# Spectral mixing and a SiLU block on one core: loads moved behind the first batch's third stage, and its stand-in products made narrow

## The chip, the cores and the metric

The kernel runs on 1 core of one Trainium2 chip. The metric is the device time of one execution in microseconds (us); lower is better. The core has a matrix engine (TensorE, PE in the profile, with its weight loads listed as PEld), VectorE (DVE), ScalarE (ACT), GpSimd (POOL) and SyncE (SP), which only issues transfers. Transfers are issued by SP, ACT or POOL and carried out by 16 DMA engines.

## The reference

Two blocks follow each other. The first mixes each channel along the sequence with a filter in the frequency domain; the second is a two-layer block with a SiLU.

```python
# x: (8, 3008, 256); filt_r, filt_i: (1505, 256)
X = np.fft.rfft(x, axis=1)
Y = X * (filt_r + 1j * filt_i)[None]
y = np.fft.irfft(Y, n=3008, axis=1).astype(np.float32)
# x: (24064, 256); w_in: (256, 2048); w_out: (2048, 256)
h = y.reshape(24064, 256) @ w_in
out = ((h / (1 + np.exp(-h))) @ w_out).astype(np.float32)
```

## The kernel before, in words

**The Fourier part** is done by small matrix products, batch by batch (B = 8), with the sequence length split as 47 x 64. Stage one (products `pa`, tiles `t1`) transforms over 94 rows, stage two (`pb`, a multiplication by the filter, `pc`) over the rest and back, stage three (`pd`) back over the rows into the tile `y` that the second block reads. Between stages the data change their layout by a trip through DRAM (`d1`, `d2`).

**The second block** runs in steps. There are 8 batches x 2 halves x 3 groups of tokens, and 8 steps (`jp`) to each group, 384 steps. `hidden(step)` makes seven products with the first weights (`px`, `pyz`, L977), the sums on VectorE and the SiLUs on ScalarE; `project(step)` makes seven products with the second weights (`acc`, L1044) one step later. Both use a scheme with seven products in place of eight, for which combinations of the weights are formed on the chip (`combine_weights`). All products are in float32; each appears in the trace as two multiplies and two weight loads.

**The weights** come as 64-bit numbers and are turned into float32 on the chip, one tile j of 16 at a time: `weights(j)` loads, `bits` takes exponent and mantissa apart (VectorE), `converted` shifts the exponent (ScalarE), `added`/`signed` (together `rounded`) and `placed` put the number together (VectorE). Step jp needs tiles 2 jp and 2 jp + 1, so that tiles 0 to 7 are prepared before the first step and 9 to 15 during the steps 0 to 6.

**The order** is written out by hand (a manual schedule): each engine carries out its instructions in the order in which the program issues them. Ahead of the steps stands a start of some 70 us, in which batch 0 goes through its stages one to three alone. `forward(0, fill=4)` puts four stand-in products in front of its own, whose result is overwritten; `idle(n)` and `idle_wide(n)` issue n stand-ins into a bank of their own, 128 or 256 columns wide. At its end the program stands like this (L1341 on): load of weight tile 9; stage-one products of batch 1 for u = 0 and 1 (`second["stage1"]`, of eight u); loads of x for u = 2 and 3 and of the weight tiles 10, 11, 12; the rest of the weight tiles 4 to 7; a copy on POOL into `gate` which holds POOL until tile 7 is placed, and behind it `store_rows`, eight transfers of t1 to d1; fifteen wide stand-ins; `stage3(g)` for g = 0 to 3, 32 products each, with their copies into y; two wide stand-ins; the load of a table `wi_t` which stage three has read until then.

From there on, work beside the steps is placed by `put(step, round, piece)`, with eight rounds to a step: the pieces are issued between the products of that step. The other `stage1(u)`, u = 2 to 7, of batch 1 stand in round 3 of the steps 0 to 5. Each issues two products (512 columns, L416), the load of x for u + 2 on SP, two copies on ScalarE (L421) into one of two `t1` buffers, and the four transfers of `store_rows` on POOL. Of d1, batch 1's stage two reads from step 10 on.

Of the kernel before, what the change touches and what calls it, by code (L numbers as in the profile page):

```python
# [263 lines left out]
def kernel(  # L264
# [9 lines left out]
    nc = tc.nc  # L274
# [65 lines left out]
    y = {}  # L340
# [18 lines left out]
    def spectral(b):  # L359
# [155 lines left out]
        def forward(g, home=(None, None), fill=0):  # L515
            t2 = None if b == 0 else t2s.pop(g)
            ps = [bank(b, f"pb_{b}_{g}_{k}", home[k]) for k in range(2)]
            for _ in range(fill):
                nc.tensor.matmul(out=ps[0][:, 0], lhsT=wx_t, rhs=wide_rows, start=True, stop=True)
            for ri in range(2):  # L520
                for j in range(4):
                    for k in range(2):
                        par, at = slot_source(k, j)
                        rows = slice(64 * par, 64 * par + 64)
                        rhs = us["t2"][rows, 2 * g + at // 2, :, at % 2] if b == 0 else t2[rows, at, :]
                        nc.tensor.matmul(out=ps[k][32 * j:32 * j + 32, ri, :],  # L526
                                         lhsT=d_t[rows, 4 * g + at, ri, :], rhs=rhs,
                                         start=True, stop=True)
            if b > 0 and g + 2 < NG:
                load_t2(g + 2)  # L530
            banks[g] = ps
            prods[g] = []
# [263 lines left out]
    def put(step, rnd, piece, *args):  # L796

        pending.append((step + rnd / ROUNDS, len(pending), lambda: piece(*args)))
# [3 lines left out]
    def plan(b, part):  # L802

        at = STEPS * b

        if b == 1:
            for u in range(2, 8):
                put(at + u - 50, 3, part["stage1"], u)
        else:
            put(at - {2: 80, 3: 120}.get(b, 128), 0, part["reverse_x"])  # L810
            early_fold = (-73, ((-68, 3), (-68, 5), (-67, 5), (-66, 5))), (-89, ((-82, 5), (-81, 3), (-81, 5), (-75, 5)))
            for f, step, load, places, ends in (
                    (0, -64, *early_fold[b > 2], ((1, 0), (1, 3))),
                    (1, -56, -63, ((-61, 5), (-60, 3), (-60, 5), (-59, 3)), ((1, 3), (2, 3))),
                    (2, -48, -55, ((-52, 3), (-52, 5), (-51, 5), (-50, 5)), ((1, 3), (2, 3)))):
                put(at + load, 4 if load == -89 else 0, part["load_fold"], f)
                for k, (fold_step, rnd) in enumerate(places):
                    put(at + fold_step, rnd, part["fold"], f, k)
                put(at + step, 7, part["stage1_fold"], f)
                put(at + step, 7, part["evict_fold"], f)  # L820
                for q, (after, rnd) in enumerate(ends):
                    put(at + step + after, rnd, part["pairs_fold"], f, q)
                joined.add(at + step)
                opened.add(at + step + 1)
            put(at - 47, 0, part["load_fold"], 3)
            for k, (step, rnd) in enumerate(((-45, 3), (-45, 5), (-44, 3), (-44, 5))):
                put(at + step, rnd, part["fold"], 3, k)
            early_out.add(at - 43)
            open_step(at - 43, (part["stage1_fold"], 3), (part["evict_fold"], 3))
            put(at - 43, 3, part["pairs_fold"], 3, 0)  # L830
            put(at - 43, 5, part["pairs_fold"], 3, 1)
            return plan_two(b, part)
        put(at - 38, 0, part["load_t2"], 0)
        put(at - 38, 0, part["load_t2"], 1)
        for g, places in enumerate((
# [6 lines left out]
            pieces = (("forward", g), ("multiply", g, 0), ("multiply", g, 1), ("add", g, 0), ("add", g, 1))  # L842
            for (step, rnd), (piece, *args) in zip(places, pieces):
                if piece != "forward" or g in (1, 3, 5):
                    put(at + step, rnd, part[piece], *args)
        open_step(at - 36, *last_part[0](5), (part["forward"], 0))
        for g, step in ((0, -32), (2, -24), (4, -16)):
            put(at + step, 7, part["inverse"], g, 2)
            if g < 4:
                pending.append((at + step + 7 / ROUNDS, 10 ** 6 + 9, lambda g=g: part["forward"](g + 2, ACCS)))  # L850
                joined.add(at + step)
            put(at + step, 7, part["even"], g, 0, 2)
            put(at + step, 7, part["even"], g, 1, 2)
            put(at + step + 1, 5, part["rows"], g, 0, 2)
            put(at + step + 2, 3, part["rows"], g, 1, 2)
        plan_rest(b, part)
# [325 lines left out]
    def add_weights(*js):  # L1182

        for j in js:
            lo, m, mo = raws[j][0], raws[j][3], raws[j][5]
            v.scalar_tensor_tensor(out=mo, in0=lo, scalar=2.0 ** -32, in1=m, op0=ALU.mult, op1=ALU.add)

    def round_weights(*js):
        for j in js:
            hi, e, eo = raws[j][1], raws[j][2], raws[j][7]  # L1190
            v.scalar_tensor_tensor(out=eo, in0=hi, scalar=0x80000000, in1=e,
                                   op0=ALU.bitwise_and, op1=ALU.bitwise_or)
# [24 lines left out]
    def weights(*js, queue=None):  # L1217
        for j in js:
            if wide:
                load_weights(j, queue)  # L1220
# [9 lines left out]
    def split(*js):  # L1230
        bits(*js)
        converted(*js)

    def rounded(*js):
        if wide:
            add_weights(*js)
            round_weights(*js)
# [25 lines left out]
    def idle_wide(n, ps=None, rhs=None):  # L1263

        ps = ps or bank(0, "idle")
        for _ in range(n):
            nc.tensor.matmul(out=ps[:, 0], lhsT=wx_t, rhs=wide_rows if rhs is None else rhs,
                             start=True, stop=True)
# [28 lines left out]
        part["stage1_first"](j)  # L1297
    second["load_two"]()
    weights(8)
    part["forward"](0, fill=4)  # L1300
    placed(0, 1)
    for g in range(1, 4):
        part["forward"](g)
# [37 lines left out]
    weights(9)  # L1341
    for u in range(2):
        second["stage1"](u, False)
    second["load_x"](2)
    weights(10)
    second["load_x"](3)
    weights(11, 12)
    converted(6, 7)
    converted(8)
    rounded(4, 5)  # L1350
    placed(4, 5)
    rounded(6, 7)
    placed(6, 7)
    gp.tensor_copy(out=gate, in_=w_t[:, 3, S3, 0, 0:1])
    for u in range(2):
        second["store_rows"](u)
    idle_wide(15)
    for g in range(4):
        part["stage3"](g)
    idle_wide(2)  # L1360
    nc.sync.dma_start(out=wi_t, in_=wi_dram.ap())
    early[0] = None
    plan_rest(0, part)
    for g in (4, 5):
# [3 lines left out]
        put(step, 0, lambda t=t, dram=dram: nc.sync.dma_start(out=t, in_=dram.ap()))  # L1368
    for b in range(1, B):
        plan(b, second if b == 1 else spectral(b))  # L1370
    def added(*js):
        if wide:
            add_weights(*js)

    def signed(*js):
        if wide:
            round_weights(*js)

    for step, rnd, *todo in (
            (0, 1, (combine_weights, 1)), (0, 5, (bits, 9), (added, 9)),  # L1380
            (1, 0, (converted, 9)), (1, 1, (added, 8), (signed, 8), (placed, 8), (signed, 9), (bits, 10)),
            (1, 2, (weights, 13)), (1, 5, (combine_weights, 2), (converted, 10)),
            (2, 1, (placed, 9), (added, 10), (signed, 10), (placed, 10), (bits, 11)),
            (2, 2, (weights, 14, 15)), (2, 5, (combine_weights, 3), (converted, 11)),
            (3, 1, (combine_weights, 4), (added, 11), (signed, 11), (bits, 12)),
            (3, 5, (placed, 11), (converted, 12)),
            (4, 1, (combine_weights, 5), (added, 12), (signed, 12), (placed, 12)),
            (4, 5, (bits, 13), (added, 13)), (5, 0, (converted, 13)),
            (5, 1, (bits, 14), (added, 14), (signed, 13), (placed, 13)),
            (5, 5, (combine_weights, 6), (converted, 14)), (5, 7, (bits, 15)), (6, 0, (converted, 15)),  # L1390
            (6, 1, (signed, 14), (placed, 14), (added, 15), (signed, 15), (placed, 15)),
            (6, 5, (combine_weights, 7))):
        for piece, *args in todo:
            put(step, rnd, piece, *args)
# [79 lines left out]
```

## Time and profile before

| | us |
|---|---|
| median of 3 runs | 2510.78 |
| lowest and highest run | 2509.8, 2512.3 |
| the profiled execution, its time | 2512.45 |
| the profiled execution, its span | 2510.7 |
| PE busy | 2488.4 (99%) |
| DVE busy | 1756.2 (70%) |
| ACT busy | 1095.5 (44%) |

The span is the time from the first to the last instruction of the core in the one execution that the profiler recorded; that execution's own time is 1.75 us longer. All times inside the execution are counted from the start of the span. A row of the timeline gives start, length, engine, line, operation, what is written and read, shapes, the number of instructions merged into the row and, in brackets, how long the engine had been idle before and what ended that. "issue" stands where the profile shows nothing that the engine waited for.

### The profile page before, as it was taken

To read this page: it belongs to the slowest core of one execution; us is meant where nothing else is said; L and a number is where in the kernel's file an instruction comes from. 1 tells how busy PE (TensorE), PEld (TensorE's weight loads), DVE (VectorE), ACT (ScalarE), POOL (GpSimd) and SP (SyncE) were. 2 spreads that over 40 slices of the span, in tenths; PEclk is the share of its full clock that TensorE was granted. 3 is DMA by queue.
4 is the path that set the end of the run, shared out by engine and by line. 5 is a ranking of instruction groups with operands and counts; after the bars stand their busy time and mean duration, and the time that the engine had idled before them with its cause. 6 is when DMAs were issued, how large, how long until landed. Compare 5 with 4: busy or idle time off the path is not lost.

```text
span 2510.7 us, 42210 instructions
## 1 busy us (share of the span) xinstructions
PE 2488.4 (99%) x16206; PEld 2133.9 (85%) x16206; DVE 1756.2 (70%) x3603; ACT 1095.5 (44%) x3006; POOL 431.0 (17%) x673
## 2 busy tenths in 40 slices
PE   8999999999999999999999999999999999999999
PEld 5688888888888888888888888888888888888988
DVE  7766777777777777777777767777677766655544
ACT  3544444444444444444444444444444444444443
POOL 3102212022121121211222112211121111101100
PEclk9999999999999999999999999999999999999999
DMA  9413232312332032420324203321042211200000
GB/s 324 147 50 95 69 92 59 81 51 73 67 86 78 27 81 59 104 70 16 93 61 109 59 25 80 86 70 43 26 109 59 55 43 34 63 21 9 17 9 17
DMA packets 139801, 170.67 MB, mean 68 GB/s; under 512 B 20860, under 2 KB 113372, under 8 KB 138716
## 3 DMA queue, kind: packets, MB, share of 16 engines
q1 hardware_dynamic: 115536, 120.77, 18.3%
q0 software_dynamic: 22080, 44.10, 6.8%
q8 instruction: 127, 2.08, 0.3%
q10 hardware_dynamic: 1984, 3.11, 0.3%
q14 instruction: 74, 0.61, 0.1%
HBM read 96.06 MB, written 81.26 MB: 71 GB/s over the span
## 4 chain that ended last, share of the span: by engine, by line
PE 97%; DVE 1%; DMA 1%; issue 0%; ACT 0%; SPq 0%; POOL 0%; DVEq 0%; ACTq 0%
PE acc L1044 45%; PE px L977 26%; PE pyz L977 19%; PE pd L754 1%; PE pf L486 1%; PE pc L582 1%; PE pb L544 1%; PE pa L392 0%; PE pa L416 0%; DMA w_t<-in_x_first_dram 0%; PE pd L718 0%; DMA w_t<-d 0%; DVE g L948 0%; PE pb L526 0%; PE pc L640 0%
## 5 line engine op out<-in xcount | busy, mean ns | idle before, releaser
L1044 PE MATMUL acc<-g,w_t 128*128 128x256 f32 (+1 forms) x5376 | 1508.2, 376 | 3.0 <-ACT o L767 2.5
L1044 PEld LDWEIGHTS acc<-g,w_t 128*128 128x128 f32 x5376 | 1017.5, 190 | 152.6 <-ACT o L767 15.3
L948 DVE TENSOR_TENSOR g<-pyz,abc 128x256 f32<-128x256 f32 (+1 forms) x1152 | 479.3, 416 | 483.3 <-ACT abc L998 241.2
L948 DVE TENSOR_TENSOR g<-g 128x256 f32<-128x256 f32 (+3 forms) x1152 | 589.7, 512 | 196.6 <-ACT g L981 183.5
L977 PE MATMUL px<-ty,w_t 128*128 128x256 f32 (+1 forms) x2304 | 676.7, 375 | 0.5 <-ACT abc L998 0.5
L981 ACT ACTIVATE g<-g 128x256 f32<-128x256 f32 (+1 forms) x1152 | 472.9, 411 | 236.9 <-DVE g L948 236.9
L948 POOL TENSOR_TENSOR s<-s 128x256 f32<-128x256 f32 (+1 forms) x329 | 252.1, 784 | 1427.5 <-DVE s L1062 1094.1
L977 PEld LDWEIGHTS px<-ty,w_t 128*128 128x128 f32 x2304 | 434.8, 190 | 56.9 <-issue 3.7
L977 PE MATMUL pyz<-y,w_t 128*128 128x256 f32 (+1 forms) x1536 | 452.1, 376 | 2.3 <-DVE g L948 2.2
L977 PEld LDWEIGHTS pyz<-y,w_t 128*128 128x128 f32 x1536 | 283.7, 189 | 46.0 <-DVE g L948 6.5
L992 ACT COPY abc<-px 128x256 f32<-128x256 f32 (+1 forms) x384 | 141.3, 368 | 373.4 <-PE px L977 373.4
L981 ACT ACTIVATE g<-px 128x256 f32<-128x256 f32 (+1 forms) x384 | 145.8, 380 | 299.7 <-PE px L977 299.7
L998 ACT COPY abc<-px 128x256 f32<-128x256 f32 (+1 forms) x384 | 141.5, 368 | 308.6 <-PE px L977 308.5
L977 PE MATMUL px<-y,w_t 128*128 128x256 f32 (+1 forms) x768 | 228.0, 379 | 0.0
L977 PE MATMUL pyz<-ty,w_t 128*128 128x256 f32 (+1 forms) x768 | 226.4, 377 | 0.2
L977 PEld LDWEIGHTS px<-y,w_t 128*128 128x128 f32 x768 | 143.8, 190 | 23.3 <-ACT g L981 2.5
L977 PEld LDWEIGHTS pyz<-ty,w_t 128*128 128x128 f32 x768 | 142.3, 190 | 21.8 <-DVE g L948 1.8
L985 ACT COPY abc<-px 128x256 f32<-128x256 f32 (+1 forms) x384 | 135.1, 352 | 36.1 <-PE px L977 36.1
L506 POOL DMA_DIRECT2D d<-tf x96 | 48.6, 506 | 216.3 <-DVE tf L436 210.8
L1062 ACT COPY s<-acc 128x512 f32<-128x512 f32 (+1 forms) x94 | 54.2, 577 | 47.6 <-issue 29.1
L603 POOL DMA_DIRECT2D d<-low x36 | 22.3, 618 | 286.3 <-DVE low L599 286.2
L476 DVE TENSOR_TENSOR uf<-x_all 120x512 f32<-120x512 f32 (+1 forms) x72 | 60.2, 864 | 0.3 <-issue 0.3
(132 smaller groups left out, 1356.5 us busy)
## 6 DMA issues: line engine op xcount, KB each, us to landing
t<-d SPq DMA_DIRECT2D x84, 256.0 KB
t<-d SPq DMA_DIRECT2D x224, 96.0 KB
out_dram<-s SPq DMA_DIRECT2D x64, 256.0 KB
d<-q POOLq DMA_DIRECT2D x48, 256.0 KB, 5.2
x_all<-in_x_dram SPq DMA_DIRECT2D x96, 96.0 KB
x_all<-xr SPq DMA_DIRECT2D x96, 96.0 KB
d<-tf POOLq DMA_DIRECT2D x96, 96.0 KB, 2.7
d<-tq POOLq DMA_DIRECT2D x96, 96.0 KB, 2.9
```

The costliest lines, as they stand in the source:

```text
L476: nc.vector.tensor_tensor(out=out, in0=in0, in1=in1, op=op)
L486: nc.tensor.matmul(out=ps[q][32 * k:32 * k + 32], lhsT=wq_t[rows, k], rhs=rhs[k][rows], start=True, stop=True)
L506: nc.gpsimd.dma_start(out=d1[par, :, grp, at:at + 4], in_=part[rows].rearrange("p q n c -> p (q n) c"))
L544: nc.tensor.matmul(out=ps[k, ri][32 * j:32 * j + 32, a, :], lhsT=dn_t[rows, 4 * (g + a) + at, :], rhs=t2s[g + a][rows, at, :], start=True, ...
L948: eng.tensor_tensor(out=out, in0=in0, in1=in1, op=op)
L977: nc.tensor.matmul(out=out, lhsT=w_t[:, jp, c, 0], rhs=rhs, start=start, stop=True, skip_group_check=True)
L981: nc.scalar.activation(out=g[:, k, 0:n], in_=g[:, k, 0:n] if src is None else src, func=AFT.Silu)
L985: nc.scalar.copy(out=sums[:, 0, 0:n], in_=xo)
L992: nc.scalar.copy(out=sums[:, 1, 0:n], in_=xo)
L998: nc.scalar.copy(out=sums[:, 2, 0:n], in_=xo)
L1044: nc.tensor.matmul(out=acc[pair][i][:, h, 0:n], lhsT=w_t[:, jp, OUT_PLACE.get(c, c), 1], rhs=g[:, k, 0:n], start=(jp == 0 and h == 0), sto ...
L1062: copy(out=s[:, 2 * i:2 * i + 2, 0:n], in_=acc[pair][i][:, :, 0:n])
```

## The change

- The loads of x for u = 2 and 3 and of the weight tiles 10, 11, 12 are issued behind stage three of batch 0, after the load of `wi_t`, in the order x(2), weights 10, 11, 12, x(3).
- Weight tile 8's `added` and `signed` are issued ahead of stage three (on VectorE in front of the copies into y); before, they stood in step 1.
- Thirty narrow stand-ins stand in front of stage three in place of fifteen wide ones; one wide one behind it in place of two; eight narrow fillers in front of `forward(0)` in place of four wide ones.
- The copy into `gate` reads a column of y that stage three's last copy writes, and stands, with the eight transfers of `store_rows` behind it, after stage three.
- `stage1(u)` of batch 1 for u = 2 to 7 stands in the steps 1 to 6 in place of 0 to 5.

```diff
@@ forward
             for _ in range(fill):
-                nc.tensor.matmul(out=ps[0][:, 0], lhsT=wx_t, rhs=wide_rows, start=True, stop=True)
+                nc.tensor.matmul(out=ps[0][:, 0, 0:128], lhsT=wx_t, rhs=wide_rows[:, 0:128], start=True, stop=True)
@@ plan
             for u in range(2, 8):
-                put(at + u - 50, 3, part["stage1"], u)
+                put(at + u - 49, 3, part["stage1"], u)
@@ the start
-    part["forward"](0, fill=4)
+    part["forward"](0, fill=8)
...
     weights(9)
     for u in range(2):
         second["stage1"](u, False)
-    second["load_x"](2)
-    weights(10)
-    second["load_x"](3)
-    weights(11, 12)
     converted(6, 7)
     converted(8)
     rounded(4, 5)
     placed(4, 5)
     rounded(6, 7)
     placed(6, 7)
-    gp.tensor_copy(out=gate, in_=w_t[:, 3, S3, 0, 0:1])
+    added(8)
+    signed(8)
+    idle(30)
+    for g in range(4):
+        part["stage3"](g)
+    gp.tensor_copy(out=gate, in_=y[0, 0][:, 0, 28:29])
     for u in range(2):
         second["store_rows"](u)
-    idle_wide(15)
-    for g in range(4):
-        part["stage3"](g)
-    idle_wide(2)
+    idle_wide(1)
     nc.sync.dma_start(out=wi_t, in_=wi_dram.ap())
+    second["load_x"](2)
+    weights(10, 11, 12)
+    second["load_x"](3)
     early[0] = None
...
-            (1, 0, (converted, 9)), (1, 1, (added, 8), (signed, 8), (placed, 8), (signed, 9), (bits, 10)),
+            (1, 0, (converted, 9)), (1, 1, (placed, 8), (signed, 9), (bits, 10)),
```

More of the change, by code (lines that the diff above doesn't have):

```diff
@@ L1232, in split, with added, signed @@
         converted(*js)
+    def added(*js):
+        if wide:
+            add_weights(*js)
+    def signed(*js):
+        if wide:
+            round_weights(*js)
     def rounded(*js):
@@ L1370 @@
         plan(b, second if b == 1 else spectral(b))
[L1371 to L1377, printed above, removed]
     for step, rnd, *todo in (
             (0, 1, (combine_weights, 1)), (0, 5, (bits, 9), (added, 9)),
-            (1, 0, (converted, 9)), (1, 1, (added, 8), (signed, 8), (placed, 8), (signed, 9), (bits, 10)),
+            (1, 0, (converted, 9)), (1, 1, (placed, 8), (signed, 9), (bits, 10)),
             (1, 2, (weights, 13)), (1, 5, (combine_weights, 2), (converted, 10)),
```

## The prediction

> **What bounds the kernel now.** I read the page first, then PE's waits over the whole span, then the chain of waits around the longest of them.
>
> ```profile
> PE 2488.4 (99%) x16206; PEld 2133.9 (85%) x16206; DVE 1756.2 (70%) x3603; ACT 1095.5 (44%) x3006; POOL 431.0 (17%) x673
> PE pd L718 <- issue: 5.5, 1, 5.5
> PE idle L1261 <- DMA wx_t<-wx_tbl: 4.8, 1, 4.8
> PE acc L1044 <- ACT o L767: 2.5, 3, 0.8
> PE pyz L977 <- DVE g L948: 2.2, 4, 0.9
> ```
>
> PE is busy 99% of the span, and apart from the start there is one wait above 0.9 us: 5.5 us in front of a stage-three product (pd, L718), put down to "issue", that is to nothing the profile shows. What is saved before the steps begin is therefore kept, because PE runs without a gap worth naming from then on. The chain of waits there (start, length, what):
>
> ```profile
> 52.76 3.84 DMA w_t<-d
> 56.74 2.63 PE pd L718 x161
> 59.36 5.48 issue
> 64.85 2.81 PE pd L718 x92
> 73.17 1.88 PE pa L416 x4
> ```
>
> Stage three of batch 0 waits for its rows (w_t<-d), runs 161 products, stops 5.48 us, and runs the last 92 at nearly double the cost of one. The windows (PE busy, PEld, DVE, ACT, POOL, granted clock, DMA share, GB/s) and the DMA view say why:
>
> ```profile
> 56.70:59.40 2.70, 2.63 (x161) 2.53 (x161) 1.77 (x3) 1.66 (x5) 0.81 (x2) 1.00 0.97 269
> 59.40:64.80 5.40, 0.00 (x0) 0.00 (x0) 0.00 (x0) 0.34 (x1) 3.60 (x8) 0.84 1.03 274
> 64.80:67.60 2.80, 2.75 (x94) 2.66 (x94) 0.55 (x1) 0.47 (x1) 0.00 (x0) 0.50 0.92 357
> 69.40:77.10 7.70, 7.18 (x19) 4.07 (x17) 3.51 (x11) 2.88 (x8) 1.16 (x2) 0.74 0.13 36
> q8 instruction: 127, 2.08, 0.3%
> q8 instruction: 1, 0.02, 16.8%
> q8 instruction: 1, 0.02, 12.1%
> ```
>
> In the hole no compute engine but POOL works, the DMA engines are full (1.03), and the clock falls to 0.50 and stays low into step 0 (0.74). Queue q8 moved 127 packets of 2.08 MB: 16.4 KB each. Each product is two weight loads and two multiplies; counting those and one instruction per extra wait, PE's stream is 32,620 instructions, so a packet is a block of 256. The second and third q8 rows are the windows 61.5 to 62.0 and 66.0 to 66.5: one block arrives inside the hole, the next right behind it. By that count stage three begins at 1,148 and the hole lies at 1,480. The block before that edge begins at 1,224: 76 instructions, or 36 multiplies, into the stage, which is near 57.1. So I read it as a late block: asked for at 57.1, begun at 61.75, usable at 64.85, 7.75 us in all, behind the loads of x and weights and POOL's stores.
>
> [...]
>
> **The change, part by part.** The sum is made on the profiled execution, 2512.45 us (span 2510.7); the median of the three runs is 2510.78, and the difference is taken off that.
>
> *Stand-ins.* Fifteen wide ones go, thirty narrow ones come:
>
> ```profile
> 49.18 6.64 PE L1267 MATMUL idle<-d_t,wx_t 96*128 96x256 f32 x30
> 4.78 7.66 PE L1261 MATMUL idle<-wx_t 96*128 96x128 f32 x36 [4.78 <-DMA wx_t<-wx_tbl]
> 11.95 0.30 PEld L1261 LDWEIGHTS idle<-wx_t 96*128 96x128 f32 x2
> 12.06 0.19 PEld L1261 LDWEIGHTS idle<-wx_t 96*128 96x128 f32 x1
> 12.17 0.28 PE L1261 MATMUL idle<-wx_t 96*128 96x128 f32 x1
> ```
>
> A wide half takes 6.64/30 = 0.22 us. Narrow ones at the start take 7.66/36 = 0.213, but their last loads, 0.19 long, start 0.11 apart (11.95, 12.06) and the multiplies follow at 12.06 and 12.17: that is the warm pace. Sixty halves at 0.108 are 6.5 us, so PE is free near 55.7, as before, with 60 instructions more. The eight narrow fillers in front of forward(0) likewise last as long as four wide ones and add 16. Together 76: stage three now begins at 1,148 + 76 = 1,224, on a block's edge, and its 516 instructions are two blocks and 4 instructions. Cost 0; if the warm pace were false, see the first rival.
>
> *Loads behind stage three.* SP now issues, after the weights of tile 9, the table wi_t, which waits for stage three's last product, and behind it x(2), weights 10, 11, 12, x(3). So these 2.3 MB (five transfers by the rows below) no longer compete with the last w_t<-d rows or with the instruction blocks; POOL's eight stores, gated on the last y copy, also move behind. Terms:
>
> The rows landed at 56.60; between the cover's end at 55.7 and 56.7 I take a start at 56.3: −0.4 (0 to −1.1). The hole goes: −5.48. The 92 products at 2.81 (30.5 ns) run as the first 161 (2.63, 16.3 ns): −1.3. New waits for blocks: one edge lies at the start of stage three, asked for some 0.9 us earlier while stand-ins run; the next is passed 256 instructions on, about 2.1 us later, and its successor is needed after another 2.1. When the hole ended at 64.85 the next packet began at 66.0, 1.15 later; the packet itself is 0.121 × 16 × 0.5 = 1.0 us; so a block takes at least 2.2 us, and by the 3.1 from packet to use in the hole at most 4.2. Against 2.1 to 3.0 available I take +0.9 in all (0 to 2.1).
>
> *pa products one step later.* Step 0 had pa and its two evictions in it:
>
> ```profile
> 71.47 0.42 DVE L948 TENSOR_TENSOR g<-pyz,abc 128x256 f32<-128x256 f32 x1 [1.48 <-PE pyz L977]
> 75.96 0.43 DVE L948 TENSOR_TENSOR g<-pyz,abc 128x256 f32<-128x256 f32 x1 [2.61 <-ACT abc L998]
> 77.70 0.42 DVE L948 TENSOR_TENSOR g<-pyz,abc 128x256 f32<-128x256 f32 x1
> 99.09 1.02 PE L1044 MATMUL acc<-g,w_t 128*128 128x256 f32 x4
> 107.13 1.02 PE L1044 MATMUL acc<-g,w_t 128*128 128x256 f32 x4
> 114.89 1.02 PE L1044 MATMUL acc<-g,w_t 128*128 128x256 f32 x4
> 121.64 1.03 PE L1044 MATMUL acc<-g,w_t 128*128 128x256 f32 x4
> 124.39 0.70 PE L977 MATMUL pyz<-y,w_t 128*128 128x256 f32 x2 [0.86 <-DVE g L948]
> ```
>
> Step 0 hangs on DVE, whose third sum at 77.70 lets step 1 go on. DVE waited 1.48 for a product at half clock and 2.61 for the copy at L998 that stood behind pa's evictions. With a warm clock and no pa, both products are there before DVE, which still has the token sums and a weight combination in hand: −4.09 at most, I take −3.8 (−2.6 if the clock stays low). In return step 6 gets the seventh pa. Steps, from one group of four to the next: 8.04 with pa, 7.76 with pa (step 5), 6.75 without (step 6). So +1.3; PE time alone is 1.88, and step 7 waits 0.86 for DVE, which would shrink: 0.2 to 1.9.
>
> *Weight tile 8* is finished earlier: two DVE operations, 1.3 us, ahead of the y copies. They go into DVE's long idle before these copies (7.55 us in front of the first one): 0; if DVE ran late, at most 1.3.
>
> *Cover of the moved transfers.*
>
> ```profile
> raw<-in_moe_w_dram SPq DMA_DIRECT2D x2, 512.0 KB
> x_all<-in_x_dram SPq DMA_DIRECT2D x1, 384.0 KB
> 66.02 0.55 DVE L732 COPY y<-pd 128x376 f32<-128x376 f32 x1 [7.55 <-PE pd L718]
> 82.86 0.42 DVE L1170 TENSOR_SCALAR e<-raw 128x512 uint32<-128x512 uint32 x1
> 81.93 0.59 ACT L421 COPY t<-pa 128x512 f32<-128x512 f32 x1 [1.15 <-PE pa L416]
> 58.53 0.19 POOL L1354 COPY gate<-w_t 128x1 f32<-128x1 f32 x1 [16.12 <-DVE w_t L1198]
> 58.77 4.23 POOL L429 DMA_DIRECT2D d<-t  x8
> d<-t POOLq DMA_DIRECT2D x8, 96.0 KB, 7.6
> ```
>
> Stage three should end near 61.3. Weights 10 are then issued near 62.2 with 0.9 MB up to their end, 3.4 us at 269 GB/s, so there near 66; step 1 reads them (82.86 before, some 10 earlier now, less two operations) near 71.6. Spare: 5 us. The eviction of pa(2) in step 1 (81.93 before for step 1, near 72 now) writes the tile of t1(0), whose four stores leave POOL by 64.3 and, at the 7.6 us of loaded stores, land at 71.9. That cover is all but used: 0 expected, up to 1 us if they run longer; ACT's copies would stand behind it, and PE behind them. SP's later issues (x(4) and on, each behind a pa) shift with their steps; the rows of d1 are read from step 10 on, over two steps behind the last store.
>
> Sum: −0.4 − 5.48 − 1.3 + 0.9 − 3.8 + 1.3 = −8.8: 2503.7 on the profiled execution, **2502.0** on the median. The bounds give −11.7 to −5.4, 2499.1 to 2505.4.
>
> **Rivals.** A difference of 0.2%, 5 us, is about what a measurement of this kernel can tell from none.
>
> 1. *Narrow stand-ins cost double.* If load and multiply followed each other at the 0.213 us of the first row above, sixty halves end at 62.0, 5.7 late, and the fillers add about 1.0: −8.8 + 6.7 = −2.1, 2508.7. For it: the mean of the 36. Against: the last starts, 0.11 apart. [...] 6%.
>
> 2. *Two late blocks in place of one: slower.* If a block takes long whatever the loads do, both edges of stage three now cost a wait. At F per block the stage ends at 54.8 + 2F; at the 7.75 seen that is 70.3 against 67.66, +2.6, with a cold clock again (DVE's 2.61 saved, not the 1.48) and +1.3 for pa: about +1.3, 2512.1. It decides from F = 7.1; over 0.2% slower needs 9.6. For it: the only hole sits on an edge. Against: the packet after the hole began in 1.15 us, not 4.65, and the dense stretch below, 322 instructions in 4.0 us and so over at least one edge, has no hole. 7%, of which 2% beyond 0.2%.
>
> ```profile
> 190.71:194.75 4.04, 4.04 (x161) 2.89 (x161) 1.65 (x4) 1.95 (x4) 3.81 (x6) 1.00 0.15 61
> ```
>
> 3. *The hole is no block at all* and stays: −8.8 + 5.5 + 1.3 − 0.9 = −2.9, 2507.9. [...] The packet in the hole and the count speak against. 3%.
>
> 4. *Transfers late.* Loads and stores together starve step 1, as above; to end over 0.2% slower it must cost 14 us, against a spare of 5 and 0. 4%.
>
> **How the numbers follow.** Forecast 80%: faster by more than 0.2%, since even its upper bound is 5.4 us below. Within 0.2%: rival 1 with 6%, rival 2 with 5%, rival 3 with 3%, together 14%. Slower: 2% of rival 2 and the 4% of rival 4. Range: the forecast's bounds, cut to 2499.3 below, where every term would have to be at its end, and stretched to 2507.0 above for blocks late by more than I allow and stores late by a few us.
>
> **What would show it.** Right: pd's 256 products in one run from about 56 to 61 with pieces of at most 2 us, clock 1.00 through step 0, no 2.61 in front of DVE's sum, sixty narrow halves in 6.5 us, step 6 near 8. Wrong: stand-ins ending near 62, an "issue" wait above 3 us in pd, clock 0.50 in step 0, or ACT waiting in step 1 on the stores' queue.

## The result, and the profile after

| | before | after |
|---|---|---|
| median, us | 2512.06 (2509.8 to 2512.5, 7 runs) | 2503.14 (2502.64 to 2504.73, 7 runs) |
| the profiled execution, its time | 2512.45 | 2503.14 |
| its span | 2510.7 | 2501.4 |

The changed kernel is faster: the ratio is 0.9967, with a 95% interval of 0.9956 to 0.9979. The forecast was 2502.0 within 2499.3 to 2507.0, and 8.8 us off the profiled execution; the profiled executions differ by 9.31 and the medians by 8.92. That 2503.14 lies 1.1 above the forecast comes of the base: the median before is 2512.06 over seven runs, and the forecast started from 2510.78 over three.

First, of the changed kernel's page, the busy time of the engines:

```profile
PE 2483.7 (99%) x16242; PEld 2129.1 (85%) x16242; DVE 1756.4 (70%) x3603; ACT 1095.6 (44%) x3006; POOL 430.9 (17%) x673
```

PE's busy time fell by 4.7 us although the page lists 36 instructions more; the rest of the 9.3 is idle time that went. PE's waits (total us, times, longest):

```profile
PE pyz L977 <- DVE g L948: 1.1, 2, 0.6
PE pd L718 <- DMA w_t<-d: 1.0, 1, 1.0
PE pd L718 <- issue: 0.8, 1, 0.8
```

The wait of 5.5 in front of a pd product is now one of 0.8. Of the waits of pyz for DVE's g two are left of four, and the longest, 0.9 before, is 0.6. The chain of waits around it (start, length, what):

```profile
51.91 5.15 DMA w_t<-d
57.20 4.01 PE pd L718 x251
61.20 0.80 issue
62.00 0.33 PE pd L718 x3
...
63.01 0.70 DVE ty L948
```

251 recorded products (each one multiply, of the two that a float32 product takes) follow each other in 4.01 us, 16.0 ns each. The one wait left stands in front of the last three. By the prediction's count stage three lies on three blocks of instructions, with four instructions in the third; three multiplies and three weight loads are left, so to within two instructions this is that block's edge. The windows of the same places (PE busy, PEld, DVE, ACT, POOL, granted clock, DMA share, GB/s):

```profile
57.17:61.20 4.03, 4.00 (x251) 3.91 (x251) 2.93 (x5) 2.17 (x5) 0.00 (x0) 1.00 0.04 12
61.20:62.00 0.80, 0.00 (x1) 0.00 (x0) 0.00 (x0) 0.00 (x0) 0.00 (x0) 1.00 0.00 0
63.00:67.80 4.80, 4.08 (x15) 2.19 (x15) 4.49 (x12) 1.89 (x6) 4.39 (x9) 1.00 0.86 264
```

The DMA engines are empty during stage three (share 0.04, then 0.00) and busy in step 0 (0.86): the transfers have moved there. The clock is 1.00 throughout. The timeline of stand-ins, of DVE and ACT in the steps 0 and 1, and of the groups of four products that end the steps 5, 6 and 7:

```profile
49.06 6.86 PE L1269 MATMUL idle<-wx_t 96*128 96x128 f32 x60
66.59 0.42 DVE L948 TENSOR_TENSOR g<-pyz,abc 128x256 f32<-128x256 f32 x1 [0.16 <-ACT abc L998]
68.34 0.42 DVE L948 TENSOR_TENSOR g<-pyz,abc 128x256 f32<-128x256 f32 x1
72.86 1.15 ACT L421 COPY t<-pa 128x512 f32<-128x512 f32 x2 [1.45 <-DMA d<-t]
74.32 0.42 DVE L948 TENSOR_TENSOR g<-pyz,abc 128x256 f32<-128x256 f32 x1 [1.39 <-ACT abc L998]
105.52 1.02 PE L1044 MATMUL acc<-g,w_t 128*128 128x256 f32 x4
113.76 1.02 PE L1044 MATMUL acc<-g,w_t 128*128 128x256 f32 x4
119.95 1.03 PE L1044 MATMUL acc<-g,w_t 128*128 128x256 f32 x4
```

DVE's wait of 2.61 in front of the second sum of step 0 is 0.16. Its third sum, on which step 1 hangs, starts at 68.34 in place of 77.70: 9.36 earlier. ACT waits 1.45 in step 1 for the stores of t1, which is one of the signs that the prediction listed under "wrong"; DVE's 1.39 behind it is no longer than where ACT waited for pa itself (1.38 with ACT's wait on pa of 1.15, in the kernel with weight tile 9 behind, below), and PE shows no wait there.

### The profile page after: what moved, and what is told of

Same layout as the page of the kernel before. It is cut to its first block, busy times and chain, and to the rows that moved or that the text cites. A ratio compares the mean times of both kernels' runs of the same rounds, so it can differ in the third digit from the quotient of the medians.

```text
span 2501.4 us, 42281 instructions
## 1 busy us (share of the span) xinstructions
PE 2483.7 (99%) x16242; PEld 2129.1 (85%) x16242; DVE 1756.4 (70%) x3603; ACT 1095.6 (44%) x3006; POOL 430.9 (17%) x673
## 4 chain that ended last, share of the span: by engine, by line
PE 97%; DMA 1%; DVE 1%; ACT 0%; issue 0%; SPq 0%; POOL 0%; DVEq 0%; ACTq 0%
PE acc L1044 46%; PE px L977 26%; PE pyz L977 20%; PE pd L754 1%; PE pf L486 1%; PE pc L582 1%; PE pb L544 1%; PE pa L392 0%; PE pa L416 0%; DMA w_t<-in_x_first_dram 0%; DMA w_t<-d 0%; DMA d<-q 0%; PE pd L718 0%; PE pb L526 0%; PE pc L640 0%; DVE g L948 0%
## 5 line engine op out<-in xcount | busy, mean ns | idle before, releaser
L998 ACT COPY abc<-px 128x256 f32<-128x256 f32 (+1 forms) x384 | 141.4, 368 | 308.6 <-PE px L977 308.5
```

The lines of the kernel that those rows point to most:

```text
L998: nc.scalar.copy(out=sums[:, 2, 0:n], in_=xo)
```

## The experiments

"Before" in each run was measured on the same chip beside it: 2512.2 to 2512.7. The ratios are to that.

### One part undone or done alone

**The loads back in front of stage three** (all else as changed).

```diff
     for u in range(2):
         second["stage1"](u, False)
+    second["load_x"](2)
+    weights(10)
+    second["load_x"](3)
+    weights(11, 12)
...
-    second["load_x"](2)
-    weights(10, 11, 12)
-    second["load_x"](3)
```

> The changed kernel with the five loads (x(2), weights 10, x(3), weights 11 and 12) put back in front of stage three; narrow stand-ins, pa one step later and the stores behind stage three stay. Theory (a late instruction block, late because of the loads): with the stage on a block's edge the second block is asked for near 55 into full queues and comes 7.75 us later, some 3 us late; the third is asked for near 62.5 and is 2 to 5 us late at the stage's end. Two waits in place of the one of 0.8, the stage ends 5 to 8 us later than in the changed kernel, the clock falls at least once: 2508 to 2512, about 2510. Rival (the place of the edge alone did it, loads do not matter): 2503 to 2504, one wait of about 0.8. Rival (the hole is no block): a hole of 5.5 at the same 164th product as before, about 2509.

Measured: 2509.88 (2508.85 to 2512.59), ratio 0.9991 (0.9982 to 1.0001). The chain:

```profile
56.27 2.09 PE pd L718 x123
58.36 0.69 issue
59.06 2.13 PE pd L718 x128
61.19 5.43 issue
66.62 0.45 PE pd L718 x3
```

Two blocks are waited for, 0.69 and 5.43 us. The long wait is back at full size, and it has moved: from behind 161 recorded products to the last three, where the changed count of stand-ins puts the edge of a block. So the wait is tied to the count of instructions, as a late block is, and its length to the transfers. The block was needed at 61.19, 2.13 us after the one before it had come into use (59.06); its packet began in the window from 64.0 to 64.25.

**Fifteen wide stand-ins again** (and four wide fillers), the loads behind.

```diff
-    idle(30)
+    idle_wide(15)
```

> The changed kernel with fifteen wide stand-ins and four wide fillers, so 76 instructions fewer in front of stage three; loads and stores behind the stage, pa one step later. Theory (late because of the loads): the edge lies 76 instructions into the stage again, the next block is asked for near 57.7 into empty queues and takes about the 2.9 us seen in the changed kernel (edge at 59.1, product after it at 62.0), so it is usable near 60.6 and needed near 59.8: one wait of 0.5 to 1.2 in front of the 164th product and none at the end, 2502.7 to 2503.7. Rival (the place of the edge did it): the hole of 5.5 us comes back, 2508 to 2510. In either case this shows what the narrow form is worth by itself.

Measured: 2503.27 (2502.47 to 2505.78), ratio 0.9966 (0.9954 to 0.9978), which is the changed kernel's time.

```profile
57.27 2.62 PE pd L718 x161
59.90 0.91 issue
60.81 1.70 PE pd L718 x93
```

The wait stands at its old place, behind 161 recorded products, and lasts 0.91 in place of 5.48. The stand-ins' form and count bring nothing once the loads are behind.

**Only pa one step later** (the kernel before, all else untouched).

```diff
-                put(at + u - 50, 3, part["stage1"], u)
+                put(at + u - 49, 3, part["stage1"], u)
```

> The kernel before with nothing changed but pa for u = 2 to 7 one step later. Theory by the trace of the changed kernel: the hole of 5.5 and the cold clock stay; DVE's wait of 2.61 in step 0 goes; step 6 grows by 1.5 and step 7 shrinks by as much, so the return costs nothing: 2.6 us less than before, about 2509.5. By the prediction's own term (pa's return costs 1.3): about 2510.8. Rival (pa does not matter, PE was busy anyway): 2512.

Measured: 2510.6 (2509.25 to 2511.25), ratio 0.9991 (0.9982 to 1.0): −2.1 us, between the −2.6 of the theory and the −1.3 of the prediction's term. In the profiled execution DVE's wait of 2.61 in step 0 is 0.34, and the hole was 6.55 us long:

```profile
57.94 2.63 PE pd L718 x161
60.57 6.55 issue
67.12 2.80 PE pd L718 x93
```

**Only the weight tiles 10 to 12 behind** (the kernel before; x(2), x(3) and the stores stay in front).

```diff
-    weights(10)
...
-    weights(11, 12)
...
     nc.sync.dma_start(out=wi_t, in_=wi_dram.ap())
+    weights(10, 11, 12)
```

> The kernel before with one thing changed: the weight tiles 10, 11, 12 are loaded behind stage three; x(2), x(3) and the stores stay in front, stand-ins and pa as before. [...] Rival (POOL's stores alone are enough to hold the block up): the hole stays above 4 us, 2511 to 2512.5.

Measured: 2509.83 (2506.79 to 2511.26), ratio 0.9989 (0.998 to 0.9998).

```profile
57.99 4.12 PE pd L718 x161
62.11 1.88 issue
64.00 1.79 PE pd L718 x93
```

And the windows ahead of them:

```profile
56.00:58.00 2.00, 0.22 (x3) 0.13 (x4) 2.00 (x5) 0.74 (x2) 0.00 (x0) 1.00 0.82 279
58.00:60.00 2.00, 2.00 (x89) 2.00 (x93) 0.61 (x2) 0.39 (x2) 1.27 (x3) 0.63 1.06 227
```

The wait fell to 1.88, but PE had waited 1.8 us for the rows before stage three, and the 161 products then ran in 4.12 us, the clock at 0.50 from 58.5 to 61.9. Of the 3.6 us that the shorter wait gave, the later start (57.99 against 56.74) took back 1.25 and the slower products 1.49; the time is above the 2505.5 to 2508.5 that I had expected of a block late in proportion to what stands in the queues.

### The place of the edges

**Two stand-ins fewer.** The edges should move out of the dense stretch.

```diff
-    idle(30)
+    idle(28)
```

> The changed kernel with 28 narrow stand-ins in place of 30, 8 instructions fewer in front of stage three. Theory: the third block's edge, now 512 instructions into a stage of 516, moves to 520, behind the stage and its wide stand-in; the wait of 0.80 in front of the last three products moves under the copies of y, which the first px waits for anyway: stage three ends 0.8 us earlier, 2502.3 (0.6 to 0.9 below the changed kernel). The cover ends 0.2 us earlier, which costs nothing, since the rows land 1 us after it. Rival (the block holds up the first px instead): 2503.1, no change.

Measured: 2504.55 (2503.29 to 2505.82), ratio 0.9969 (0.9957 to 0.998): no gain, against the expectation.

```profile
57.68 2.13 PE pd L718 x127
59.81 1.18 issue
60.99 2.13 PE pd L718 x127
63.54 1.18 issue
```

Now two blocks are waited for, 1.18 us each; the second wait stands behind the stage, in the middle of its wide stand-in. The first block's packet began in the window from 58.50 to 58.75, over 1 us after the stage's start at 57.39, and was used at 60.99; the second began at 62.0 to 62.25 and was used at 64.72. In the profiles with the edge at the stage's first instruction the first packet began earlier, from 1.9 us before the stage's first product (54.0 in the changed kernel) to some 0.5 behind it (56.25 to 56.50, loads in front). A reading that fits is that the next block is asked for only when the instruction at the edge is reached, which with the edge eight instructions into the stage lies behind one that has to wait for the rows. That is not shown: PE has no wait for the rows in this profile, where the stand-ins ended late. The waits differ by 1.6 us (2.36 against 0.80), the medians by 1.0 to 1.4, which the intervals don't separate.

### The stores and the place of pa

**Gate and stores in front again**, all else as changed:

```diff
-    gp.tensor_copy(out=gate, in_=y[0, 0][:, 0, 28:29])
-    for u in range(2):
-        second["store_rows"](u)
...
     placed(6, 7)
+    gp.tensor_copy(out=gate, in_=w_t[:, 3, S3, 0, 0:1])
+    for u in range(2):
+        second["store_rows"](u)
     added(8)
```

> The changed kernel with POOL's gate on the weights and the eight stores in front of stage three again, as before the change; all else as changed. Theory: the stores (0.8 MB, near 58.8 to 63) stand in the queues when the third block is asked for near 59.2: the wait of 0.8 at the stage's end grows to 1.5 to 3, 2504 to 2505.5. ACT's wait of 1.45 for these stores in step 1 goes and brings nothing, since PE had no wait there. Rival (only the loads count): 2503.1. Rival (ACT's wait cost something): 2502.

Measured: 2503.43 (2503.05 to 2505.32), ratio 0.9967 (0.9955 to 0.998): by the medians the stores' place alone is worth nothing (2503.58 for the changed kernel on the same chip). The profiled execution took 2505.32, within the theory's 2504 to 2505.5, with a block wait of 1.41 and half clock behind it; but its stage three also began late, at 57.80.

**pa back in the steps 0 to 5**, all else as changed (`put(at + u - 50, ...)`):

> The changed kernel with pa for u = 2 to 7 back in steps 0 to 5; loads behind the stage and the rest as changed. Theory: x(2), issued at 62.7, is there near 65.8, so the product in step 0 waits little, but its evictions hold the copy at L998 and with it DVE: 2.6 to 3.5 us more at step 1; step 6 shrinks by 1.5 and step 7 grows by as much: 2505.7 to 2506.6. By the prediction's term (pa's return costs 1.3): 2504.4 to 2505.3. Rival (in step 0 pa fills what PE waits anyway): 2503.1.

Measured: 2512.76 (2509.82 to 2514.35), ratio 1.0002 (0.9992 to 1.0011). I had missed by over 6 us. ACT's timeline and PE's wait:

```profile
73.47 1.07 ACT L421 COPY t<-pa 128x512 f32<-128x512 f32 x2 [6.40 <-DMA d<-t]
74.87 1.22 PE L977 MATMUL px<-ty,w_t 128*128 128x256 f32 x2 [4.79 <-ACT abc L998]
```

The copy of pa(2) overwrites the tile that the stores of t1(0) read. These stores now leave behind stage three, and so ACT's copy of pa(2) in step 0 waits 6.40 us for them, the copy at L998 stands behind it, and PE waits 4.79 behind that. The one part is worth 2.1 us in the kernel before and 9.2 with the loads and stores behind: pa's shift is not a part beside the others but what makes room for them. The 9.2 include the clock, too, which was at 0.50 for 3.4 us from 62.5 and for 6.8 from 72.7. The first of these stands behind a block wait, as the chain shows:

```profile
57.99 0.51 issue
58.50 2.13 PE pd L718 x128
60.63 1.87 issue
```

Here the rows were in time, and two blocks are waited for with hardly a transfer about: the DMA share is 0.03 from 58.50 to 60.63 and 0.00 in the wait. The second block took 4.0 us from the use of the one before to its own (58.50 to 62.50), against 7.56 with the loads in front.

**pa back, the stores in front.** This takes the stores' wait out.

> The changed kernel with the copy into gate and the eight stores of t1 in front of stage three, and pa's products of u = 2 to 7 back in the steps 0 to 5. With pa in step 0 and the stores behind stage three, ACT waited 6.4 us in step 0 for the stores of t1 and the kernel took 2512.8. Theory (what cost so much there was the landing of the stores, not pa itself): the wait d<-t in front of the copy t<-pa in step 0 is gone or below 1 us, and pa in step 0 costs two products and two copies, 2 to 3 us, less the 0 that its going from step 6 is worth: 2505.0 to 2507.0. Rival A (pa in step 0 costs what it cost before whatever the stores do, ACT's copies standing in front of those of step 0): 2508 to 2513 with no wait on d<-t. Rival B (the stores are late there, too, because they go out in front of stage three beside the last rows): the wait stays over 3 us.

Measured: 2510.54 (2507.5 to 2513.16), ratio 0.9991 (0.9982 to 1.0). The wait for the stores is gone, and the time is still 3.5 us above what I had expected, where rival A had it. In the profiled execution, which took 2508.13, DVE waits 3.12 in step 0 for the copy at L998. PE's timeline, and the step of the chain that ends at 76.31:

```profile
66.75 1.98 PE L416 MATMUL pa<-x_all,wx_t 96*128 96x512 f32 x4 [0.60 <-DMA x_all<-in_x_dram]
76.44 1.96 PE L416 MATMUL pa<-x_all,wx_t 96*128 96x512 f32 x4 [1.72 <-DMA x_all<-in_x_dram]
```

```profile
64.09 12.22 DMA x_all<-in_x_dram
```

Something else had been hidden by pa's later place: x(3), last of the five transfers, takes 12.22 us from its issue and is late by 1.72 for pa(3) in step 1; x(2) is late by 0.60 in step 0.

**The same with x(3) ahead of the weights.**

```diff
     second["load_x"](2)
-    weights(10, 11, 12)
     second["load_x"](3)
+    weights(10, 11, 12)
```

> As the run before with the stores in front of stage three and pa of u = 2 to 7 in the steps 0 to 5, and the load of x(3) ahead of the weight tiles 10 to 12 as well. There PE waited 1.72 us in step 1 for x(3), the last of five transfers, and the time was 2510.5. Theory (each of the things that stage one of batch 1 reads or overwrites was covered by its standing one step later): with x(3) second of the five the 1.72 is gone, the wait for x(2) in step 0 stays near 0.6, and 2507.5 to 2509.5 remains, of which a block wait above 1.3 us and the half clock behind it are some 2. Rival (pa in step 0 costs by itself, because ACT's copies of pa stand ahead of the copy that DVE waits for): DVE's wait on that copy in step 0 stays near 3 us, and the time is 2509.5 to 2511.5.

Measured: 2509.48 (2506.7 to 2511.23), ratio 0.9986 (0.9977 to 0.9995), where the two expectations meet, so the rows have to decide. PE's and DVE's timeline:

```profile
70.02 1.98 PE L416 MATMUL pa<-x_all,wx_t 96*128 96x512 f32 x4 [1.23 <-DMA x_all<-in_x_dram]
72.93 0.42 DVE L948 TENSOR_TENSOR g<-pyz,abc 128x256 f32<-128x256 f32 x1 [3.44 <-ACT abc L998]
```

The wait of step 1 is gone, as the theory had it. But DVE waits 3.44 in step 0 although the clock is 1.00 there, as the rival had it: 1.23 of it is x(2), the rest pa's products and the two copies. From the first token sum to the third g takes 8.58 us here (66.09 to 74.67), 9.32 in the kernel before (68.38 to 77.70), 5.33 in the changed one (63.01 to 68.34). The 8.58 include the 1.23 for x(2), which was not late in the kernel before. So of the 3.99 that step 0 lost, some 2.0 to 3.25 are pa's going and the rest the clock; with only pa moved the stretch is 5.82 (70.65 to 76.47), mostly at full clock, and the two can't be separated further. What else lies between 2509.5 and 2503.4 in the medians isn't settled: in the profiled executions 1.2 us are a later start of stage three (58.42 against 57.20) and about 1.5 its first 251 products, at half clock behind PE's wait of 1.7 for the rows (5.46 against 4.01), and nothing ties either to pa.

### A version beyond

**Weight tile 9 behind stage three, too**, ahead of x(2):

```diff
-    weights(9)
...
     nc.sync.dma_start(out=wi_t, in_=wi_dram.ap())
+    weights(9)
     second["load_x"](2)
```

> The changed kernel with the load of weight tile 9 moved, too: behind stage three, after the table wi_t and ahead of x(2). Theory: the last rows of stage three take 5.15 us from issue to landing while the 512 KB of tile 9 go out behind them; alone they take some 3 us, PE's stand-ins end at 55.9 and stage three starts near 56.0 in place of 57.2: 2502.0 to 2502.8, and DVE's step 0, which takes tile 9 apart at 66.9, still finds it there, near 66. Rival A (rows and instruction blocks were not held up by tile 9): the rows land at 57.0 as before and the time stays at 2503.4, within 0.5. Rival B (tile 9 comes too late): DVE waits in front of its operation on raw in step 0 or 1, and the time is 2504 or more.

Measured: 2502.66 (2502.29 to 2503.46), ratio 0.9962 (0.9949 to 0.9976). The chain:

```profile
56.00 4.14 PE pd L718 x253
60.14 0.86 issue
```

DVE's timeline, where it takes tile 9 apart:

```profile
66.30 0.43 DVE L1170 TENSOR_SCALAR e<-raw 128x512 uint32<-128x512 uint32 x1 [0.29 <-DMA raw<-in_moe_w_dram]
```

Stage three starts at 56.00, where the stand-ins end, and tile 9 is late by only 0.29 for DVE. It is the lowest time of all. The changed kernel, run once more beside other kernels, took 2503.58 (2502.87 to 2504.24), ratio 0.9966 (0.9954 to 0.9979):

> The changed kernel as it is, for the comparison of these runs on one chip: every theory expects its ratio to the kernel before again, 0.9967, about 9 us below it.

So the gain over the changed kernel is 0.5 to 0.9 us, on other chips, and the ranges overlap: likely, not shown.

**Tile 9 behind and the stores in front.**

> Both: weight tile 9 loaded behind stage three and the stores of t1 in front of it. The stores then go out beside nothing but the last rows, and nothing but loads is left behind stage three. If tile 9 is what holds the rows up: 2501.8 to 2502.8, with the stores' place worth nothing, as it was alone. If stores hold the rows up when tile 9 doesn't: 2503.0 to 2504.5. If the block of instructions in stage three is late because of the stores (1.41 us there with the stores alone in front): its wait is 1.2 to 1.5 again, and the time is 2503 to 2504.

Measured: 2503.78 (2503.01 to 2508.74), ratio 0.9969 (0.9958 to 0.9981). Its stores run beside tile 9. The chain, and DVE's timeline:

```profile
63.78 5.72 DMA raw<-in_moe_w_dram
```

```profile
69.60 0.43 DVE L1170 TENSOR_SCALAR e<-raw 128x512 uint32<-128x512 uint32 x1 [1.53 <-DMA raw<-in_moe_w_dram]
```

The load takes 5.72 us in place of 4.48, and DVE waits 1.53. That speaks for leaving the stores behind stage three, as the changed kernel has them, once tile 9 is behind; the ranges of the two runs overlap (2502.29 to 2503.46 without the stores in front), so it is likely, not shown.

## Why the prediction was right, point by point

The profiled executions, term by term:

| term | predicted | measured | from |
|---|---|---|---|
| start of stage three | −0.4 (0 to −1.1) | +0.46 | 56.74 to 57.20 |
| the hole | −5.48 | −5.48 | gone |
| products at half clock | −1.3 | −1.10 | 2.63 + 2.81 to 4.01 + 0.33 |
| new waits for blocks | +0.9 (0 to 2.1) | +0.80 | one wait |
| DVE's waits in step 0 | −3.8 | −3.99 | 9.32 to 5.33 |
| pa's return in step 6 | +1.3 (0.2 to 1.9) | 0.0 | below |
| sum | −8.8 | −9.3 | |

- **The late block**: shown. The wait goes with the transfers (5.43 with the loads in front, 0.80 to 1.87 with loads and stores behind) and stands, to within a few instructions, where the count puts an edge, in three kernels with three counts. The block of 256 in that count is the prediction's estimate from 32,620 instructions and 127 packets, 257 to a packet. Its 7.75 us from asking to use take the block as asked for when the one before it comes into use; that, too, is an estimate, and no run shows when a block is asked for. From the use of one block to the use of the next it took 7.56 with the loads in front again (59.06 to 66.62), with them behind 2.9 in the changed kernel (about 59.1 to 62.00, the 59.1 by the count) and 4.0 with pa back. So the loads make some 3.6 to 4.7 us of it, and the rest is there without them. The term of 0.9 for new waits fits the 0.80 here and the 1.13 of the changed kernel's other profile; the 0.51 and 1.87 with pa back are more than its bound of 2.1.
- **Which part does it**: the loads, given the rest: 2509.9 with them in front, 2503.1 to 2503.6 behind. Within the stand-ins, alignment and form brought nothing (2503.27 with wide ones), as the prediction's cost of 0 had it. Rival 1 was wrong: sixty halves took 6.86 us, 0.114 each, a little over the 0.108 taken, and hidden by the wait for the rows. Their weight loads take 0.19 each, and the products still go at 0.114, so that load and multiply do not wait for each other here, as the rival had them do.
- **The start** had the wrong sign. The step that failed is that less traffic brings the rows earlier. In the profiles with tile 9 in front, stage three started anywhere from 55.94 to 58.42, with loads behind and in front alike (55.98 with them in front, 58.42 with them behind). One profiled execution can't show a term of 0.4 there. A part of the spread comes from the very start of the program, which the change leaves alone: in four profiles (only pa moved, two stand-ins fewer, the stores in front, tile 9 and the stores moved) PE waited 1.42 to 1.66 us near 12 for the first x, the clock then was at 0.50 for 3.4 us, and the stand-ins ended at 57.4 to 58.1 in place of about 56. That tile 9 holds the rows up isn't shown: without it in front the stage started at 56.00, with it in front once at 55.94.
- **pa's return** was mis-sized: I took step 6's growth and let go of what follows. Step 6 grew from 6.75 to 8.24 (105.52 to 113.76), and step 7 shrank from 7.67 to 6.19 (113.76 to 119.95), because DVE, for which step 7 had waited twice (0.86 and 0.23), caught up during pa: no such wait is left. The prediction names step 7's wait of 0.86 as what would shrink, but lets it take away only that much. This mistake of 1.3 us and the one of 0.86 in the start have opposite signs, so that the sum came within 0.5 us is in part luck.
- **The cover of the moved transfers** (the work that hides their time) held, but thinner than worked out. The prediction had the stores' landing near 71.9 just meet the copy of pa(2) near 72. The copy started at 72.86, behind the stores, so these landed some 0.9 later. ACT waited 1.45; as it waits 1.15 for pa itself where the stores are no hindrance (tile 9 behind), the stores cost ACT about 0.3 and PE nothing. That cover exists because pa had moved. With pa in step 0 the same stores cost 4.8 us of PE, and with the stores in front x(2) and x(3) up to 1.7 each. The prediction priced the parts as if they added up; they add up in this order only.
- **Rivals 2 and 3**: one block edge, not two, cost a wait, and it was short (0.80); the hole went with the transfers. The edge that the count puts 256 instructions into the stage left no gap in the changed kernel (251 products in one run, 16.0 ns each); where a block was waited for, the edge cost 0.51 to 6.55 us. Rival 4 happened on ACT and stopped there.

## What to carry to other kernels

A stall that the profile puts down to nothing, with full DMA queues and at a fixed count of instructions (here 5.48 us at a DMA share of 1.03), can be a block of instructions behind data transfers: move bulk loads that nobody needs soon behind the dense stretch (here 0.80 us were left), and look where the instruction count puts the next edges. When transfers are moved later, list for each what reads its target and what overwrites its source, and move those users as well; here the shift of pa was worth 2.1 us alone, and without it the whole lost 6 to 9 us (of the 6, with the stores in front, only about half is traced to rows). Work that is put into a step behind an engine that lags is paid for only as far as that engine doesn't catch up in the next one; here step 6 grew by 1.49 us and step 7 shrank by 1.48.

## What the hardware showed that I had not expected

- From the start of a block's packet to its first instruction it took about 2.2 to 3.1 us: 2.8 to 3.1 in the kernel before (from 61.75 to 62.0, used at 64.85) and with x(3) first (62.0 to 62.25, 65.08), 2.2 to 2.7 in the changed kernel (59.5 to 59.75, 62.00, and in its other profile 59.25 to 59.5, 61.98), with the stores in front (60.75 to 61.0, 63.24), with the loads in front (64.0 to 64.25, 66.62) and with two stand-ins fewer (both packets). What varied is the time from the use of the block before to the packet: some 0.5 us in the changed kernel, 1.5 with pa back (58.50 to 60.0, hardly a transfer about), 4.9 with the loads in front (59.06 to 64.0).
- Behind block waits of 0.80 to 1.20 us in this stage the clock stayed at 1.00. Behind 1.34 (stores in front, pa back) and 1.41 (stores in front) it fell to 0.50, about 1 us after PE had gone on, and with 1.87 (pa back) as PE went on. But behind the 1.72 us in front of pa(3) it stayed at 1.00, so that the length of the gap alone doesn't decide. At the program's start it is alike: waits of 0.36 to 1.10 for the first x left the clock up in nine profiles, those of 1.42 to 1.66 in four profiles had half clock behind them, and one of 1.44 (wide stand-ins) had not. Windows of the kernel with pa back and the stores in front (the granted clock is the third number from the end):

```profile
62.00:63.00 1.00, 0.90 (x3) 0.50 (x2) 0.90 (x2) 0.22 (x1) 1.00 (x3) 0.70 0.62 159
63.00:64.00 1.00, 1.00 (x4) 0.67 (x2) 0.93 (x3) 0.27 (x1) 1.00 (x3) 0.50 0.97 181
65.00:66.00 1.00, 1.00 (x3) 0.50 (x2) 0.97 (x4) 0.56 (x2) 0.00 (x0) 0.60 0.97 332
76.00:77.00 1.00, 0.56 (x2) 0.35 (x3) 0.00 (x0) 0.00 (x0) 0.00 (x0) 1.00 0.74 287
```

  Windows inside the phase show 0.50, those around it 1.00. Taken as a mix of the two, a mean of 0.70 is 0.6 us at half clock and one of 0.60 is 0.8 us, so that by this estimate the half clock lasted from 62.4 to 65.8, 3.4 us. In the kernel with the stores in front it is 3.4 us again (64.26 to 67.68), and in the one with x(3) first (58.34 to 61.74). Longer phases were about two and three times as long: 6.8 us with the loads in front (65.4 to 72.2) and 10.2 in the kernel before (63.1 to 73.3). Why the clock stayed up behind the gap of 1.72 is not shown.
